# Joining 67 of 367 transfers in a four-layer FFT kernel, with a planner that knows the eight completion semaphores

## The chip, the cores and the metric

The kernel runs on one core of a Trainium2 chip. The core has a matrix engine (TensorE, called PE in the profile, with PEld for its weight loads), VectorE (DVE), ScalarE (ACT), GpSimd (POOL) and SyncE (SP), and 16 DMA engines that move data between HBM and the on-chip memories SBUF and PSUM. Each engine executes its own instructions in the order of the program and waits on semaphores for the others. The metric is the device time of one execution in microseconds (us); lower is better.

## The reference, cut to what matters

The input `x` has shape 1 x 2048 x 512 and is float32. Four layers are applied in turn, A, B, A, B, each with a layer norm ahead of it and added to its input:

```python
def A(x):                       # GFNet: a filter in the frequency domain
    return irfft2(rfft2(x, axes=(-2, -1)) * (w_r + 1j * w_i), s=(S, D))

def B(u):                       # S4: a long convolution per channel
    K = einsum("dn,dnl,dn->dl", C, exp(dt * A * arange(L)), dt * B).real
    y = irfft(rfft(pad(u.T, 2 * L)) * rfft(pad(K, 2 * L)), 2 * L)[:, :L]
    return y.T + u * Dskip

x = x + A(layernorm(x))
x = x + B(layernorm(x))
x = x + A(layernorm(x))
x = x + B(layernorm(x))
```

S = L = 2048, D = 512, and the state of B has 128 complex numbers per channel. The weights of both A layers are the same, and so are those of both B layers, so that the spectrum of K is computed once.

## The kernel before

All Fourier transforms are matmuls with small tables, done in two steps (a table of 16 or 64 points, a transposition through memory, a second table that also holds the twiddle factors). `x` (16 tiles of 128 x 512), and two large work areas `Y` and `Ya`, stay in SBUF; `wk` is an area that is cut into rings of small buffers (`RING1`, `RING2`: name, width in float32 per partition, number of buffers). PSUM is used as banks of 512 columns.

The work is cut into pieces, each a Python generator of the class `Net`. The ones that matter here:

- `first_a(r, g)` and `group_a(g)`: the column transform of A, the product with the weights and the inverse, for group g of 16. Each loads a table (`cPa`, `cGa`) and its weights (`W1`, `W`) with a transfer of its own, into one buffer `G`. `inv_a(r, s2)` is the last step of A for one of 16 tiles; in the first layer it loads `x` again (L732, 256 KB per tile), since the tile was used as workspace.
- `exp_k`, `unit_k` build the kernel K (L1127 and L1187 on PE, L1143 Exp and L1157 to L1163 Sin on ACT, L1159 to L1171 on DVE, L1174 on POOL). ACT has one function table at a time: the profile shows an `ACT_TABLE_LOAD` where Exp, Sin and the Sqrt of the layer norm (L498) follow each other. `store_k(q)` stores a quarter of K to HBM (`kd`), and `turn_k(q, i)` loads it transposed (L1235, four loads of 256 KB with 512-byte runs), does the first step of its transform (L1253 on PE), copies the result (L1268 DVE, L1270 ACT) and stores it to `yk` (L1274, issued on ACT). The last quarter is handled within layer B, with `load_t`.
- `spectra_k(q)` loads `yk` (L837, two of 256 KB), does the second step (L826 on PE, by `spectrum`), copies (L846) and stores the spectrum to `khat` (L847, on ACT, two of 256 KB).
- `forward_b(r, b, e)`: layer norm and first step of B's transform (L793 on PE, L795 on ACT) for one half e of the channels; the result goes to `Y` (e = 0) or `Ya` (e = 1) by a transfer that is issued by SP for even b and by ACT for odd b (L811). `group_b(r, q, e)`: second step (L826), product with `khat` (L921 on DVE, L927 on POOL), back (L938 on PE, L947 on ACT). In the first B layer, e = 1, it also makes the second half of the spectrum from `yk` (L898, L906, L907) with tables that `load_g` has loaded (L866, eight of 128 KB). `inv_b(r, b, e)`: the rows come back by L957 (SP for even b, ACT for odd b), then L965 on PE, L971 on DVE.

What sets the order: the class `Clock` is a list scheduler that runs while the program is built. Every `yield` of a piece names the engines and the ring buffers that its next step needs. `time` says when they will be free, `run` takes, among the steps that are ready within 0.1 us of the earliest, the one with the lowest rank, and `note` moves the planner's clocks on by a cost per instruction (`COST`), and for a transfer by its bytes at a fixed rate plus a fixed landing time. The program order that results is then fixed.

One rule is not in the planner before the change. There are eight completion semaphores for transfers (the program calls them `DMAHW0` to `DMAHW7`; below: lanes). The transfers of both issuing queues, SP's and ACT's, take them in turn, in program order. A transfer can therefore be issued only when the eighth one ahead of it, from whichever queue, has landed. An ACT issue that waits for this holds up all that follows on ACT, its computation too.

## Time and profile before

| | |
|---|---|
| time, median of 3 runs | 803.64 us (803.43 to 808.02) |
| time of the profiled execution | 801.81 us |
| its span, first to last instruction | 800.0 us |
| granted TensorE clock, mean | 0.944 |
| PE busy | 648.6 us (81%) |
| DVE busy | 510.2 us (64%) |
| ACT busy | 419.5 us (52%) |
| POOL busy | 306.5 us (38%) |
| DMA | 132.51 MB, mean 166 GB/s |
| transfers in the program | 367 |

The profile is one execution, taken by the hardware profiler. Its page gives the busy time of each engine, the span in 40 slices of 20 us, the DMA queues, the chain of work that ended last, and the costliest groups of instructions. A row of a timeline has the start, the busy time, the engine, the line of the kernel, the operation, output <- inputs, the shape and a count; the bracket at its end is the idle time of that engine just ahead, with what ended it. `ACTq` and `SPq` are the issues of transfers on these two queues. The row names an output by its area (`wk`, `Y`, `Ya`, `x`, `ps` for PSUM).

### The profile page before, as it was taken

The page shows a single profiled execution, that of the slowest core. Times are in us where ns is not written, and L with a number is a line of the kernel's source. Part 1 is how long each engine was busy: PE and PEld are TensorE (multiplying, and loading weights), DVE is VectorE, ACT ScalarE, POOL GpSimd, SP SyncE. Part 2 cuts the span into 40 slices and gives each one's busy share as a digit, 9 for nine tenths or more (in the row PEclk, how much of TensorE's full clock was granted, in tenths as well). Part 3 has the DMA queues.
Part 4 walks back from the last instruction along what each step waited for, and adds up shares of the span by engine and source line. Part 5 has one row for each costly group of instructions (what it writes and reads, how often), then busy time and mean ns, then how long its engine had stood idle before and what let it go on. Part 6 is the DMA issues. An engine that isn't in the chain of part 4 may idle for free. (4 is left out here: it accounts for less than half of the span.)

```text
span 800.0 us, 23463 instructions
## 1 busy us (share of the span) xinstructions
PE 648.6 (81%) x9892; PEld 419.3 (52%) x9892; DVE 510.2 (64%) x1022; ACT 419.5 (52%) x767; POOL 306.5 (38%) x339
## 2 busy tenths in 40 slices
PE   4389888967899799888858887889887898788796
PEld 4377555535456344346423453777665554444465
DVE  5975667747748594885525454886767588466532
ACT  5765898886886957845232324175533233433130
POOL 4290336516425340320314325264544554075420
PEclk9699999997999999999898999999997999999999
DMA  9217212630624668547986783940664524866839
GB/s 325 60 59 274 89 47 84 192 96 14 217 80 151 233 205 244 181 133 165 259 219 194 193 246 131 255 174 1 232 218 139 186 56 107 186 195 160 257 89 281
DMA packets 85960, 132.51 MB, mean 166 GB/s; under 512 B 5756, under 2 KB 57728, under 8 KB 85216
## 3 DMA queue, kind: packets, MB, share of 16 engines
q1 hardware_dynamic: 51424, 93.26, 38.3%
q10 hardware_dynamic: 34432, 37.76, 16.6%
q8 instruction: 78, 1.28, 0.7%
q14 instruction: 26, 0.21, 0.1%
HBM read 70.31 MB, written 27.13 MB: 122 GB/s over the span
## 5 line engine op out<-in xcount | busy, mean ns | idle before, releaser
L1174 POOL TENSOR_TENSOR Y<-wk,Y 128x1024 f32<-128x1024 f32 x32 | 64.8, 2027 | 120.5 <-issue 70.6
L927 POOL TENSOR_TENSOR wk<-wk 128x512 f32<-128x512 f32 x32 | 40.0, 1274 | 111.5 <-DVE wk L921 110.4
L965 PE MATMUL ps<-wk,cRbT 64*128 64x256 f32 x512 | 61.4, 384 | 5.5 <-DMA wk<-Ya 3.5
L921 DVE TENSOR_TENSOR wk<-ps,Y 128x512 f32<-128x512 f32 x64 | 39.5, 682 | 40.7 <-PE ps L826 34.8
L795 ACT COPY wk<-ps 128x512 f32<-128x512 f32 x64 | 37.1, 587 | 52.7 <-PE ps L793 45.4
L1159 DVE SCALAR_TENSOR_TENSOR wk<-wk,ps 128x1024 f32<-128x1024 f32 x32 | 38.9, 1216 | 40.5 <-ACT wk L1157 40.4
L793 PE MATMUL ps<-wk,cRb 128*32 128x256 f32 x1024 | 60.1, 380 | 4.4 <-DVE wk L515 2.8
L1127 PE MATMUL ps<-wk,Y 96*128 96x512 bf16 x128 | 44.0, 422 | 24.1 <-DVE Y L1170 13.9
L938 PE MATMUL ps<-wk,Y 32*32 32x256 f32 x1344 | 40.0, 415 | 24.7 <-ACT Y L947 9.3
L965 PEld LDWEIGHTS ps<-wk,cRbT 64*128 64x128 f32 x512 | 51.8, 187 | 15.1 <-issue 5.6
L558 PE MATMUL ps<-cRa,wk 128*128 128x256 f32 x128 | 36.6, 411 | 28.1 <-POOL wk L540 24.8
L921 DVE TENSOR_TENSOR Y<-ps,wk 128x512 f32<-128x512 f32 x64 | 39.6, 683 | 26.1 <-issue 17.5
L793 PEld LDWEIGHTS ps<-wk,cRb 128*32 128x32 f32 x1024 | 37.9, 109 | 28.2 <-DVE wk L515 3.4
L1187 PEld LDWEIGHTS ps<-Y 128*32 128x32 f32 x2048 | 36.4, 125 | 27.8 <-issue 12.8
L1143 ACT ACTIVATE Y<-ps 128x1024 f32<-128x1024 f32 x48 | 46.3, 1030 | 7.3 <-PE ps L1127 7.1
L1187 PE MATMUL ps<-Y 128*32 128x64 f32 x2048 | 42.0, 243 | 9.1 <-ACT wk L676 2.5
L947 ACT COPY Ya<-ps 128x256 f32<-128x256 f32 x64 | 19.3, 385 | 56.5 <-PE ps L938 42.9
L1170 DVE TENSOR_TENSOR Y<-ps,Y 128x1024 f32<-128x1024 f32 x32 | 39.0, 1218 | 13.0 <-ACT ps L1163 12.9
L742 PE MATMUL ps<-cDaT,apart 128*32 128x256 f32 (+1 forms) x256 | 46.3, 328 | 0.5 <-DVE x L770 0.3
L971 DVE TENSOR_TENSOR x<-x,ps 128x256 f32<-128x256 f32 x64 | 24.8, 408 | 32.9 <-PE ps L965 32.8
L540 POOL TENSOR_TENSOR wk<-wk 128x256 f32<-128x256 f32 x32 | 25.9, 808 | 49.6 <-ACT wk L513 43.9
L927 POOL TENSOR_TENSOR wk<-Y 128x512 f32<-128x512 f32 x22 | 27.5, 1276 | 45.1 <-DVE Y L921 40.1
(218 smaller groups left out, 1649.9 us busy)
## 6 DMA issues: line engine op xcount, KB each, us to landing
yk<-wk ACTq DMA_DIRECT2D x32, 256.0 KB
wk<-khat SPq DMA_DIRECT2D x16, 512.0 KB
Y<-in_W_dram SPq DMA_DIRECT2D x12, 515.0 KB
x<-in_cPa_dram SPq DMA_DIRECT2D x16, 384.0 KB
Y<-in_cGa_dram SPq DMA_DIRECT2D x12, 384.0 KB
x<-in_W_dram SPq DMA_DIRECT2D x16, 258.0 KB
x<-in_A_x_dram SPq DMA_DIRECT2D x8, 512.0 KB
kd<-wk SPq DMA_DIRECT2D x4, 1024.0 KB
```

The costliest lines, as they stand in the source:

```text
L742: nc.tensor.matmul(p[32 * i:32 * i + 32, o:o + n], self.folded(r, i)[:, b, s2].rearrange("p g m -> p (g m)"), self.DaT[:, b, first:first + ...
L793: self.nc.tensor.matmul(p[o:o + 32, 256 * h:256 * h + 256], self.Rb[:, 2 * h + j, 32 * a:32 * a + 32], xn[s], start=True, stop=True)
L921: nc.vector.tensor_tensor(t[c][:, j], x, kh[:, j, ::-1, :] if c else kh[:, j], op=OP.mult)
L927: nc.gpsimd.tensor_tensor(Z[:, :, c], t[0][:, :, c], t[1][:, :, c], op=op)
L938: nc.tensor.matmul(v[j][h][i:i + 32], gi[o:o + 32, j, 4 + 2 * s + c, :], Z[o:o + 32, j, c, :], start=c == 0, stop=c == 1)
L965: nc.tensor.matmul(q[s], self.RbT[o, i, :], y[o, i, :], start=i == 0, stop=i == 3)
L1127: self.nc.tensor.matmul(p, f[:, c:c + 128], self.oh[:k, o:o + 512], start=True, stop=True)
L1143: nc.scalar.activation(m[:, :, 1024:] if i == 2 else m[:, i, :1024], p.rearrange("p (i m) -> p i m", i=2) if i == 2 else p, AF.Exp)
L1159: nc.vector.scalar_tensor_tensor(s, c, MAGIC, p, op0=OP.subtract, op1=OP.subtract)
L1170: nc.vector.tensor_tensor(E[:, 1, :1024], p, m[:, :1024], op=OP.mult)
L1174: nc.gpsimd.tensor_tensor(E[:, 0, :1024], c, m[:, :1024], op=OP.mult)
L1187: nc.tensor.matmul(pk[32 * j:32 * j + 32, 64 * e:64 * e + 64], E1[:, r, i, :], E2[:, r, i], start=r == 0, stop=r == 1)
```

## The change

Two things are changed together.

First, 67 of the 367 transfers are joined with a neighbour. Table and weights of a group of A lie in one array on the host and come with one load (17 `PA`, 15 `GA`); `x` is loaded again two tiles at a time (8 of 512 KB for 16 of 256 KB); `turn_k` takes its input from a new piece, `load_kt`, with two loads of 512 KB (1 KB runs) for four; `spectra_k` has one load of 512 KB for two and one store of 512 KB for two; `load_g` loads its eight tables by 4, 3 and 1. The rings `KT` and `yh` have two buffers of 1024 for four of 512.

Second, the planner keeps the landing times of the last eight transfers (`self.lanes`). In `note` a transfer starts no earlier than the first of them; in `time` a step that needs SP waits for as many of them as it has transfers on SP. A transfer on ACT is moved on in `note` alone. The planner also measures a buffer's place by the size of its type.

```diff
-RING1 = {"yd": (1024, 5), "oh": (1280, 1), "KS": (2048, 1), "KT": (512, 4), "yh": (512, 4), "gb": (256, 3), "st": (256, 2), "sk": (128, 1)}
+RING1 = {"yd": (1024, 5), "oh": (1280, 1), "KS": (2048, 1), "KT": (1024, 2), "yh": (1024, 2), "gb": (256, 3), "st": (256, 2), "sk": (128, 1)}
...
+        self.lanes = last.lanes if last else [0.0] * 8
...
                 both = all(str(a.space) != str(DRAM) for a, _ in aps)
+                start = max(start, self.lanes[0])
                 self.land = max(self.land, start) + out.nbytes() / RATE[both]
                 done = self.land + LAND
+                self.lanes = self.lanes[1:] + [done]
...
-            ready = max([ready, *(self.free.get(k, 0.0) for k in words if k in COST)])
+            ready = max([ready, *(self.free.get(k, 0.0) for k in words if k in COST), *self.lanes[:words.count("SP")]])
...
-        nc.sync.dma_start(ca, self.io["cGa"][g])
+        nc.sync.dma_start(G, self.io["GA"][g])
         W = G[:, 768:1796].rearrange("p (r s f) -> p r s f", r=2, s=2)
-        nc.sync.dma_start(G[:, 768:1798], self.io["W"][g])
...
-        yield "SP" if not r else "PE", self.after(("group", r), 16)
-        if not r:
-            nc.sync.dma_start(xs, self.io["A_x"].rearrange("b (p s) d -> p (b s) d", p=128)[:, s2, :])
-            self.mark("again", s2)
+        yield "SP" if not r and s2 % 2 == 0 else "PE", self.after(("group", r), 16)
+        if not r and s2 % 2 == 0:
+            two = slice(s2, s2 + 2)
+            nc.sync.dma_start(self.x[:, two, :], self.io["A_x"].rearrange("b (p s) d -> p (b s) d", p=128)[:, two, :])
+            self.mark("again", s2 // 2)
...
-        for j in range(2):
-            nc.sync.dma_start(y[j], self.yk[0, 2 * q + j].rearrange("c a b h d -> (c a b) h d"))
+        nc.sync.dma_start(y.rearrange("p g h d -> p g (h d)"), self.yk[0, 2 * q:2 * q + 2].rearrange("g c a b h d -> (c a b) g (h d)"))
...
         for j in range(2):
-            nc.scalar.copy(kh[j].rearrange("p r d -> p (r d)"), p[j])
-            nc.scalar.dma_start(self.khat[:, 2 * q + j, :, :256], kh[j])
+            nc.scalar.copy(kh[:, j].rearrange("p r d -> p (r d)"), p[j])
+        nc.scalar.dma_start(self.khat[:, 2 * q:2 * q + 2, :, :256], kh)
...
-    def load_g(self, q):
+    def load_g(self, q, n):
...
+        nc.sync.dma_start(self.wk[:, o:o + 256 * n].rearrange("p (q m) -> p q m", q=n),
+                               self.io["cGk"][q:q + n].rearrange("q p a b m -> p q (a b m)"))
...
+    def load_kt(self, q, i):
+
+        nc = self.nc
+        yield "SP KT", self.after(("stored", q))
+        t = self.kt[q, i] = self.w("KT", [128, 4, 256])
+        self.timer.keep(t)
+        nc.sync.dma_start(t, self.kd[q].rearrange("j (a s) d -> a j (s d)", s=16)[:, :, 256 * i:256 * i + 256])
...
-            KT = self.w("KT", [128, 4, 128])
-            nc.sync.dma_start(KT, kd[:, :, 128 * i:128 * i + 128])
+        KT = self.KT3[:, :, 128 * i:128 * i + 128] if last else self.kt[q, i // 2][:, :, 128 * (i % 2):128 * (i % 2) + 128]
...
-        for q in range(8):
-            yield 0, self.load_g(q)
+        for q, n in ((0, 4), (4, 3), (7, 1)):
+            yield 0, self.load_g(q, n)
```

The order of the instructions moves where the planner decides otherwise. POOL keeps its order. DVE, ACT and PE differ in the stretches that lie, by the times of before, at about 148 to 180 us, 224 to 272 us, 290 to 366 us, 409 to 428 us and 452 to 472 us; from about 475 us on these three engines keep theirs, and only SP's list has the joined loads. The lines of after are 3 to 16 higher than those of before (L811 is L814, L947 is L955, L1270 is L1284, L1274 is L1288, L826 is L829, L938 is L946, L965 is L973).

ACT where the last quarter of K is transformed, beside the first group of `group_b` (about 404 to 428 us). `Ya<-wk` is a store of `forward_b`, `yk<-wk` one of `turn_k`, and `Y<-ps` the copy that empties the PSUM banks of L938. Before:

```order
L795 COPY wk<-ps 128x512 x4
L811 DMA Ya<-wk 16x8x1024
L947 COPY Y<-ps 128x256 x4
L795 COPY wk<-ps 128x512 x2
L1274 DMA yk<-wk 512x1x128
L811 DMA Ya<-wk 16x8x1024
L1274 DMA yk<-wk 512x1x128
L947 COPY Y<-ps 128x256 x4
L1270 COPY wk<-ps 128x4x128
L1274 DMA yk<-wk 512x1x128 x2
L947 COPY Y<-ps 128x256 x4
```

and now:

```order
L798 COPY wk<-ps 128x512 x4
L814 DMA Ya<-wk 16x8x1024
L955 COPY Y<-ps 128x256 x4
L798 COPY wk<-ps 128x512 x2
L1288 DMA yk<-wk 512x1x128 x2
L955 COPY Y<-ps 128x256 x4
L1284 COPY wk<-ps 128x4x128
L1288 DMA yk<-wk 512x1x128
L955 COPY Y<-ps 128x256 x4
L1288 DMA yk<-wk 512x1x128
L1284 COPY wk<-ps 128x4x128
L1288 DMA yk<-wk 512x1x128 x2
```

The second `Ya<-wk`, which stood between the two stores to `yk`, now comes behind all of these rows, as the next one.

ACT at the last spectra of the first half and the transform of the third quarter of K (about 279 to 310 us); `khat<-wk` is the store of `spectra_k`. Before:

```order
L1157 ACTIVATE wk<-ps,magic 128x1024
L846 COPY wk<-ps 128x512
L847 DMA khat<-wk 128x2x256
L846 COPY wk<-ps 128x512
L847 DMA khat<-wk 128x2x256
L1157 ACTIVATE wk<-ps,magic 128x1024
L746 COPY wk<-ps 128x512
L1162 ACTIVATE wk<-wk,quarter 128x1024
L1163 ACTIVATE ps<-wk 128x1024
```

and now:

```order
L1165 ACTIVATE wk<-ps,magic 128x1024
L848 COPY wk<-ps 128x512 x2
L849 DMA khat<-wk 128x4x256
L1165 ACTIVATE wk<-ps,magic 128x1024
L749 COPY wk<-ps 128x512
L1170 ACTIVATE wk<-wk,quarter 128x1024
L1171 ACTIVATE ps<-wk 128x1024
```

Two stores became one, behind both copies. Some 10 rows further on, ACT has now a pair of Sin instructions with a table load of its own (`L1170 ACT_TABLE_LOAD`) between the Sqrt of the layer norm and the Exp group; this pair stood ahead of the Sqrt before, so that ACT has one table load more in all.

PE at the rows that come back for layer B (about 450 to 472 us); L965 is the matmul of `inv_b`. Before:

```order
L826 MATMUL ps<-wk 32x256 x16
L938 MATMUL ps<-wk,Y 32x256 x32
L826 MATMUL ps<-Ya,Y 32x256 x16
L965 MATMUL ps<-wk,cRbT 128x256 x32
L938 MATMUL ps<-wk,Y 32x256 x32
L826 MATMUL ps<-wk 32x256 x16
L938 MATMUL ps<-wk,Y 32x256 x32
L826 MATMUL ps<-Ya,Y 32x256 x16
L965 MATMUL ps<-wk,cRbT 128x256 x8
L938 MATMUL ps<-wk,Y 32x256 x32
```

and now:

```order
L829 MATMUL ps<-wk 32x256 x16
L973 MATMUL ps<-wk,cRbT 128x256 x8
L829 MATMUL ps<-Ya,Y 32x256 x16
L973 MATMUL ps<-wk,cRbT 128x256 x24
L946 MATMUL ps<-wk,Y 32x256 x32
L829 MATMUL ps<-wk 32x256 x16
L946 MATMUL ps<-wk,Y 32x256 x32
L829 MATMUL ps<-Ya,Y 32x256 x16
L946 MATMUL ps<-wk,Y 32x256 x64
L973 MATMUL ps<-wk,cRbT 128x256 x8
```

The first 32 L965 are split in 8 and 24, and the first L938 moved behind them; further on 8 L965 changed places with 32 L938.

More of the change, by code (lines that the diff above doesn't have):

```diff
@@ L265, in boxes @@
         step = min([a for a, _ in rest], default=1)
+        size = mybir.dt.size(ap.dtype) / 4
         return [(p, max(1, s // width), n, low * size, step * size, (low + span) * size) for low in lows]
@@ L666, in first_a @@
         ca = G[:, :768].rearrange("p (a b) -> p a b", a=6)
-        nc.sync.dma_start(ca, self.io["cPa"][g])
+        nc.sync.dma_start(G, self.io["PA"][g])
         W = G[:, 768:1284].rearrange("p (a b) -> p a b", a=2)
-        nc.sync.dma_start(W, self.io["W1"][g])
         yield "PE p:t y", self.after(("forward", r), 16), *((self.emitted(("loaded", 0, 1), 8),) if r else ())
@@ L764, in inv_a @@
         self.drop(Y4)
-        yield "DVE" if r else ("DVE", self.after(("again", s2)))
+        yield "DVE" if r else ("DVE", self.after(("again", s2 // 2)))
         two = xs.rearrange("p (a b) -> p a b", a=2)
@@ L831, in spectra_k @@
         nc = self.nc
-        yield "SP KT KT gb", self.after(("turn", 0), 8)
+        yield "SP KT gb", self.after(("turn", 0), 8)
         gb = self.w("gb", [128, 2, 4, 32])
         nc.sync.dma_start(gb, self.io["cGk"][q])
-        y = [self.w("KT", [128, 2, 256]) for _ in range(2)]
-        for j in range(2):
-            nc.sync.dma_start(y[j], self.yk[0, 2 * q + j].rearrange("c a b h d -> (c a b) h d"))
-        yield "PE p:k yh yh"
-        kh = [self.w("yh", [128, 2, 256]) for _ in range(2)]
+        y = self.w("KT", [128, 2, 2, 256])
+        nc.sync.dma_start(y.rearrange("p g h d -> p g (h d)"), self.yk[0, 2 * q:2 * q + 2].rearrange("g c a b h d -> (c a b) g (h d)"))
+        yield "PE p:k yh"
+        kh = self.w("yh", [128, 2, 2, 256])
         p = self.psum("k")
         p = p[:, :512], p[:, 512:]
-        self.spectrum(gb, y, p)
-        self.drop(gb, *y)
+        self.spectrum(gb, [y[:, j] for j in range(2)], p)
+        self.drop(gb, y)
         yield "ACT"
         for j in range(2):
-            nc.scalar.copy(kh[j].rearrange("p r d -> p (r d)"), p[j])
-            nc.scalar.dma_start(self.khat[:, 2 * q + j, :, :256], kh[j])
+            nc.scalar.copy(kh[:, j].rearrange("p r d -> p (r d)"), p[j])
+        nc.scalar.dma_start(self.khat[:, 2 * q:2 * q + 2, :, :256], kh)
         self.mark("khat", q)
@@ L859, in tables @@
             self.mark("gi", r, q)
-    def load_g(self, q):
-        yield "SP gk", self.emitted(("rows", 0, 1), 8)
-        gk = self.gk[q] = self.w("gk", [128, 2, 4, 32])
-        self.timer.keep(gk)
-        self.nc.sync.dma_start(gk, self.io["cGk"][q])
-        self.mark("gk")
-        yield self.emitted("gk", q + 1)
+    def load_g(self, q, n):
+        yield "SP" + " gk" * n, self.emitted(("rows", 0, 1), 8)
+        t = [self.w("gk", [128, 2, 4, 32]) for _ in range(n)]
+        o = t[0].offset % WORK
+        for i in range(n):
+            self.gk[q + i] = t[i]
+            self.timer.keep(t[i])
+            assert t[i].offset % WORK == o + 256 * i
+        self.nc.sync.dma_start(self.wk[:, o:o + 256 * n].rearrange("p (q m) -> p q m", q=n),
+                               self.io["cGk"][q:q + n].rearrange("q p a b m -> p q (a b m)"))
+        for _ in range(n):
+            self.mark("gk")
+        yield self.emitted("gk", q + n)
     def early(self, q):
@@ L1222, in load_t @@
         self.mark("last")
+    def load_kt(self, q, i):
[4 more added lines that the diff above has]
+        nc.sync.dma_start(t, self.kd[q].rearrange("j (a s) d -> a j (s d)", s=16)[:, :, 256 * i:256 * i + 256])
+        if i == 0:
+            yield "+SP sk"
+            self.sk[q] = self.w("sk", [1, 128])
+            self.timer.keep(self.sk[q])
+            nc.sync.dma_start(self.sk[q], self.io["B_Dskip"].rearrange("(q a d) -> q a d", q=4, a=1)[q])
+        self.mark("kt", q, i)
     def turn_k(self, q, i):
         nc = self.nc
-        kd = self.kd[q].rearrange("j (a s) d -> a j (s d)", s=16)
         last = q == 3
-        if last:
-            yield self.emitted("last")
-            KT = self.KT3[:, :, 128 * i:128 * i + 128]
-        else:
-            yield "SP KT", self.after(("stored", q))
-            KT = self.w("KT", [128, 4, 128])
-            nc.sync.dma_start(KT, kd[:, :, 128 * i:128 * i + 128])
-        if i == 0:
-            if last:
-                sk = self.sk3
-            else:
-                yield "SP sk"
-                sk = self.w("sk", [1, 128])
-                nc.sync.dma_start(sk, self.io["B_Dskip"].rearrange("(q a d) -> q a d", q=4, a=1)[q])
-            yield ("DVE", self.after("last")) if last else "DVE"
-            o = KT[0:1, :, 0:32]
+        came = "last" if last else ("kt", q, i // 2)
+        yield self.emitted(came)
+        KT = self.KT3[:, :, 128 * i:128 * i + 128] if last else self.kt[q, i // 2][:, :, 128 * (i % 2):128 * (i % 2) + 128]
+        if i == 0:
+            yield "DVE", self.after(came)
+            o, sk = KT[0:1, :, 0:32], self.sk3 if last else self.sk[q]
             nc.vector.tensor_tensor(o, o, sk.rearrange("p (j d) -> p j d", j=4), op=OP.add)
-        yield ("PE p:x p:x", self.after("last")) if last else "PE p:k"
+            if not last:
+                self.drop(sk)
+        yield "PE p:x p:x" if last else "PE p:k", self.after(came)
         if last:
@@ L1252, in turn_k @@
         for h in range(2):
-            nc.tensor.matmul(p[h], self.Rk[:, h, :], KT if last else KT.rearrange("p j m -> p (j m)"), start=True, stop=True)
-        if not last:
-            self.drop(KT)
+            nc.tensor.matmul(p[h], self.Rk[:, h, :], KT, start=True, stop=True)
+        if not last and i % 2:
+            self.drop(self.kt[q, i // 2])
         for h in range(2):
             if not last:
-                yield "ACT yh"
-                r = self.w("yh", [128, 4, 128])
+                yield "ACT" if h else "ACT yh"
+                y = y if h else self.w("yh", [128, 2, 4, 128])
+                r = y[:, h]
             elif not h:
@@ L1275, in turn_k @@
                                 .rearrange("g c a d -> (g c) a d"), r)
-            if not last:
-                self.drop(r)
+            if not last and h:
+                self.drop(y)
             yield "+"
@@ L1287, in plan_k @@
         M, KS = {}, {}
+        self.kt, self.sk = {}, {}
         self.F, self.th = self.w("F", [128, 2, 2, 512]), self.w("th", [128, 512])
@@ L1303, in plan_k @@
                 for i in range(4 if b < 7 else 0):
+                    if i % 2 == 0:
+                        yield 4 * b + 6 + i, self.load_kt(b // 2, i // 2)
                     yield 4 * b + 6 + i, self.turn_k(b // 2, i)
@@ L1475 @@
     arrays = {"A_x": np.ascontiguousarray(A_x), "B_Dskip": np.ascontiguousarray(B_Dskip),
-              "W": host_w(A_w_r, A_w_i), "W1": host_w1(A_w_r, A_w_i),
               **host_k(B_A_re, B_A_im, B_B_re, B_B_im, B_C_re, B_C_im, B_log_dt),
               **tables_a(), **tables_b(), **table_k()}
+    for name, table, w in (("GA", "cGa", host_w(A_w_r, A_w_i)), ("PA", "cPa", host_w1(A_w_r, A_w_i))):
+        arrays[name] = np.concatenate([arrays.pop(table).reshape(16, 128, 768), w.reshape(16, 128, -1)], 2)
     nc = bacc.Bacc("TRN2", target_bir_lowering=False, num_devices=1, dynamic_dma_scratch_size=4096)
```

## The prediction

> **What bounds the kernel now.** I read the page's busy times and slices first, then the waits of PE, then the timeline at the longest wait that the change touches.

> ```profile
> span 800.0 us, 23463 instructions
> PE 648.6 (81%) x9892; PEld 419.3 (52%) x9892; DVE 510.2 (64%) x1022; ACT 419.5 (52%) x767; POOL 306.5 (38%) x339
> PEclk9699999997999999999898999999997999999999
> DMA  9217212630624668547986783940664524866839
> ```

> PE is busy for 648.6 of 800.0 us (so it waits for 151), and no other engine comes near it in most slices. The end follows PE, so time is won where PE waits or where its clock is below full, and a transfer saved elsewhere is worth nothing. The waits of PE by what ended them (sum, times, longest):

> ```profile
> PE ps L558 <- POOL wk L540: 24.8, 3, 13.1
> PE ps L1127 <- DVE Y L1170: 13.9, 7, 3.2
> PE ps L938 <- ACT Y L947: 9.7, 5, 8.3
> PE ps L826 <- DMA Y<-wk: 6.3, 2, 3.2
> PE ps L965 <- DMA wk<-Ya: 3.5, 5, 0.9
> PE ps L1127 <- DMA wk<-in_cGk_dram: 1.8, 1, 1.8
> ```

> The largest is the start, which the edit leaves as it is. Direct waits on transfers are small, and hardly any is on a transfer that gets joined (`Y<-wk` and `wk<-Ya` stay as they are). So what the joins save on SP and on the DMA engines is mostly hidden already. The one long wait in the middle is on a copy of ACT, 8.3 us. The timeline there:

> ```profile
> 405.93 5.58 SPq L895 DMA_DIRECT2D Y<-khat  x4
> 408.19 1.50 PE L938 MATMUL ps<-wk,Y 32*32 32x256 f32 x64
> 408.94 0.68 ACTq L811 DMA_DIRECT2D Ya<-wk  x1
> 409.61 1.98 PE L1253 MATMUL ps<-wk,cRk 128*128 128x512 f32 x4
> 411.56 2.83 SPq L866 DMA_DIRECT2D wk<-in_cGk_dram  x3
> 418.84 0.53 ACTq L1274 DMA_DIRECT2D yk<-wk  x1
> 419.41 1.20 ACT L947 COPY Y<-ps 128x256 f32<-128x256 f32 x4 [10.50 <-DMA Ya<-wk]
> 419.92 2.91 PE L938 MATMUL ps<-wk,Y 32*32 32x256 f32 x64 [8.33 <-ACT Y L947]
> 422.76 3.78 PE L1253 MATMUL ps<-wk,cRk 128*128 128x512 f32 x4
> ```

> The copies at 419.41 need only PE's L938 of 408.19. What held ACT is the issue ahead of them: the `yk` store at 418.84 waits for the `Ya` store of 408.94, which lies on the lane that this store gets, and which takes 9.9 us because four loads of 512 KB from `khat` went out around it. PE, whose PSUM banks wait for the copies, stands still for 8.33 us, and then runs slowly. The same stretch in windows of 4 us (PE, PEld, DVE, ACT, POOL, granted clock, DMA share, GB/s):

> ```profile
> 408.00:412.00 4.00, 3.59 (x76) 1.50 (x68) 1.29 (x3) 0.59 (x1) 2.49 (x2) 1.00 1.02 231
> 412.00:416.00 4.00, 0.00 (x0) 0.00 (x0) 0.33 (x1) 0.00 (x0) 0.00 (x0) 1.00 1.11 311
> 416.00:420.00 4.00, 0.08 (x4) 0.11 (x8) 0.00 (x0) 0.59 (x3) 0.00 (x0) 0.53 1.06 293
> 420.00:424.00 4.00, 4.00 (x66) 2.35 (x67) 0.00 (x0) 2.30 (x8) 0.00 (x0) 0.50 1.04 308
> 424.00:428.00 4.00, 4.00 (x59) 1.59 (x66) 0.93 (x2) 0.59 (x1) 0.00 (x0) 0.69 0.06 16
> 428.00:432.00 4.00, 2.64 (x56) 0.75 (x40) 4.00 (x8) 0.00 (x0) 1.58 (x2) 1.00 0.50 135
> ```

> The granted clock falls to 0.53, 0.50 and 0.69 behind the idle stretch, and the DMA engines are full until 424 us and nearly idle after.

> **Part 1, 409 to 426 us.** In the new order on ACT both `yk` stores come ahead of the copies, and the `Ya` store behind all six `yk` stores. Counting eight back in the new program, the first `yk` store behind the copies gets the lane of a `Ya` store that SP issues before its `khat` loads, the next two those of `yk` stores of the same stretch, the next that of the first `khat` load. None of these is the late `Ya` store. So the wait of 8.33 us goes, and with it the slow stretch: L938 x64 took 2.91 us where it took 1.50 before the stop (1.41), and L1253 x4 3.78 for 1.98 (1.80). Together 8.33 + 1.41 + 1.80 = 11.5 us, the upper end.

> What is late next is the `khat` data. The windows from 408 to 424 move 4 x (231 + 311 + 293 + 308) = 4.57 MB, and the next products, L921 on DVE, need the first two of the four loads. Each 512 KB takes 1.7 to 2.3 us at these rates; going by the order of issue I estimate the second at 418 us and the last at 421 (between 414 and 424). With PE 11.5 us earlier DVE wants the second at about 418.6 and the last two from about 421. That is just met; with the `yk` stores, which now share the DMA engines (256 KB each, 0.9 us at 293 GB/s), it may be missed by 0 to 5 us. I take 1.5, the nearer to "just met": **-10** (-11.5 to -6). The `Ya` store that was moved back is wanted by L826 only here:

> ```profile
> 446.33 1.36 PE L826 MATMUL ps<-Ya,Y 64*32 64x256 f32 x32
> ```

> That is 27 us behind the copies of 419.41; with the 9.9 us that it took it is still early. If its own lane, that of the second `khat` load, isn't free, ACT stops there for about a microsecond, with the 16 copies of the next group behind it; PE comes to the banks of these some 4 us later, so this is covered.

> [...]

> **Part 2, 253 to 345 us.** Here `spectra_k`, the reload of `x` and the building of K run side by side. Stretch, busy times as above:

> ```profile
> 148.00:253.00 105.00, 86.07 (x1231) 52.53 (x1230) 71.35 (x109) 81.79 (x100) 47.00 (x35) 0.92 0.35 109
> 253.00:345.00 92.00, 79.00 (x1256) 38.77 (x1248) 63.87 (x114) 68.51 (x86) 29.45 (x20) 0.96 0.66 211
> 280.00:300.00 20.00, 19.42 (x310) 9.51 (x308) 18.07 (x37) 10.14 (x14) 8.21 (x6) 0.92 0.63 205
> ```

> ```profile
> 282.75 0.37 ACTq L847 DMA_DIRECT2D khat<-wk  x1
> 283.16 0.59 ACT L846 COPY wk<-ps 128x512 f32<-128x512 f32 x1 [1.86 <-DMA x<-in_A_x_dram]
> 285.91 1.12 ACT L1157 ACTIVATE wk<-ps,magic 128x1024 f32<-128x1024 f32 x1 [2.16 <-DMA x<-in_A_x_dram]
> 299.74 1.28 ACT L498 ACT_TABLE_LOAD   x1 [0.59 <-ACT wk L1270]
> ```

> ACT loses two waits of its `khat` stores for loads of `x` (1.86 and 2.16; with eight loads for sixteen the eighth one ahead is older). Sixteen `khat` stores become eight; at 0.37 us for an issue that is 8 x 0.37 = 3.0. One table load comes in, 1.28. On ACT that is 1.86 + 2.16 + 3.0 - 1.28 = 5.7 us. But PE is busy for 19.42 of the 20 us around these waits, so there they cost nothing; PE's idle time in the whole stretch is 92 - 79 = 13 us, and ACT, with 68.5 of 92, is only sometimes what it waits for. I take a third, **-2**. Ends: if all of ACT's time is on the path and a clock dip goes with it, -7; if the table load and its pair of Sin instructions come between PE and the Exp group, +3 (1.28, and a dip of 1.5 us as at 474 us in part 4). The loads for `turn_k` are fewer and of the same bytes, behind the same loads of `x`; no PE wait on them is among the waits above.

> **Part 3, 148 to 253 us.** PE is busy for 86.07 of 105 and ACT for 81.79. Some unit steps change places; no wait of a lane is removed here and no work added but the joins. The waits for L1170 above are up to 3.2 us, and could move either way: **0** (-4 to +3), one such wait with its dip.

> **Part 4, 440 to 475 us.** L965 is split, and L938 comes later or earlier by one group.

> ```profile
> 440.00:476.00 36.00, 29.65 (x670) 17.01 (x670) 17.43 (x36) 9.87 (x26) 10.58 (x9) 0.93 0.84 237
> 454.33 1.37 PE L938 MATMUL ps<-wk,Y 32*32 32x256 f32 x50 [1.43 <-issue]
> 467.52 1.49 PE L938 MATMUL ps<-wk,Y 32*32 32x256 f32 x64
> 474.15 2.40 PE L938 MATMUL ps<-wk,Y 32*32 32x256 f32 x64 [2.19 <-POOL wk L927]
> 476.48 1.67 PE L826 MATMUL ps<-wk 64*32 64x256 f32 x32
> 477.94 1.08 PE L826 MATMUL ps<-Ya,Y 64*32 64x256 f32 x32
> ```

> At 454 PE stands before an L938 while L965 could have run, 1.43 us. In the new order it runs. The wait of 2.19 at 474 cost more than itself: 2.40 for 1.49 and 1.67 for 1.08 follow, so 2.19 + 0.91 + 0.59 = 3.7. Against a gain: DMA is at 0.84, and rows that come back later would hold the early L965. I take **-1** (-4 to +2).

> [...]

> **The rest.** The joined `GA` and `PA` loads save 32 issues on SP; no wait of PE for them is among the waits listed, and the weights, which came last, still do. The cover is the lead of several groups; without it the later landing of a 900 KB load would cost a microsecond or two per group. From 475 us on the three compute engines keep their order: **0** (-0.5 to +1).

> **Sum.** -10 - 2 + 0 - 1 + 0 = -13 on 801.81: 788.8. The median of the runs shown is 803.64, 1.8 above the profiled execution, so 790.6 for a median.

> **Rivals.**

> *The gain at 411 us is given back.* DMA is above 1.0 from 408 to 424, so what it carries ends no earlier. If the next stage waits for it, PE's hole only moves behind L826, and keeps the dip: of 11.5 us some 3 remain, the rest is -3: 803.6 - 6 = 798. For it: four loads of `khat` sit in that queue. Against: the DMA share is 0.06 right after, and only half the loads are wanted at once.

> *The other stretches gain too.* If the upper ends of parts 2 to 4 come half true (-3.5 - 2 - 2) with -11.5, it is -19: 784.6. For it: many waits of 2 to 3 us each with a slow stretch behind. Against: ACT's gain lies where PE is busy.

> *Joined transfers pay by themselves.* If fixed costs of transfers were on the path, all waits of PE for DMA in the list (6.3 + 3.5 + 1.8 = 11.6) could go: 790.6 - 11.6 = 779. Against: those transfers aren't joined. [...]

> *A new wait for a lane on ACT: slower.* The planner makes only steps on SP wait for lanes before it picks them; ACT's issues are picked as before. A joined load holds its lane longer, and where an ACT store lands eight behind one in a full stretch (440 to 475 us, share 0.84; or 345 to 404), the event of 418.84 comes back with its price of 11.5 us. One such takes the gain away (790.6 + 11.5 = 802), two make it slower: 813.6. It decides when ACT's wait outlasts PE's supply, a few us. For it: the stores of L957 and L907 on ACT stand there close behind loads. Against: ACT is busy for 9.87 of 36 us there, so it has room.

> *The change doesn't do what it says*: the late lane is met by another of the stores, and the wait stays. Then 803.6 - 3 = 800.6.

> **How the numbers follow.** Forecast (faster, 786 to 795): 0.48. More gains: 0.14. Joins pay: 0.03. Given back: 0.12, half of it above 795.6. Not done: 0.06. New wait on ACT: 0.17, of it 0.07 about level and 0.10 slower. One per cent of 803.64 is 8 us, about what a measurement of this kernel can tell from no change; so faster means under 795.6, slower over 811.7. Faster: 0.48 + 0.14 + 0.03 + 0.06 = 0.71; within: 0.06 + 0.06 + 0.07 = 0.19; slower: 0.10. The range takes in the forecast with the ends of its parts and both milder rivals: 778 to 804.

> **What would show it.** Right: no `yk` store on ACT with a wait of several us near 410, L938 behind it at 1.5 us for 64, granted clock 1.0 in that stretch, L1253 of the last quarter ending 10 us earlier relative to the stretch before; the waits of `khat` stores for `x` gone; ACT's busy time about 1 us more by the table load. Wrong: a wait of L921 on `Y<-khat` of over 3 us, a new wait of ACT on a DMA of over 3 us, or PE waits for L1143 behind the moved Sin pair. The prediction falls if the stretches before 400 us, whose order moved most, differ by more than 5 us.

## The result, and the profile after

The changed kernel takes 794.6 us in the median of 20 runs, the one before 803.3 us. The ratio is 0.988, with a 95% interval of 0.986 to 0.991 (all ratios leave out runs over 1.5% above the fastest of their kernel: 4 of these 20, 2 of 6 on the second occasion, 5 of the 10 of `joins_only` below). On the second occasion, on one chip with the kernel before, it was 0.982 (0.978 to 0.986). The profiled execution has a span of 788.8 us, 11.2 less than before; a single execution of this kernel may lie 10 us off another. The forecast was 790.6 in a range of 778 to 804.

The page after: busy times, and waits of PE by what ended them (sum, times, longest). L829 is L826 of before, L946 is L938, L955 is L947, L1135 and L1178 are L1127 and L1170.

```profile
span 788.8 us, 23367 instructions
PE 651.1 (83%) x9892; PEld 420.5 (53%) x9892; DVE 508.4 (64%) x1022; ACT 419.9 (53%) x768; POOL 304.1 (39%) x339
```

```profile
PE ps L829 <- issue: 14.8, 7, 4.6
PE ps L1135 <- DVE Y L1178: 10.3, 5, 2.5
PE ps L946 <- ACT Y L955: 1.5, 4, 0.4
PE ps L946 <- issue: 1.0, 2, 0.9
```

The same kind of rows before:

```profile
PE ps L938 <- issue: 9.5, 6, 2.5
PE ps L826 <- issue: 2.2, 2, 1.3
```

The 8.3 us behind ACT's copy are gone (9.7 in all before, 1.5 now). L826 on "issue", 2.2 us before, is now the second largest, 14.8 us; but L938 on "issue" went from 9.5 to 1.0, and one of the seven waits in the 14.8 (4.07 us at 687.05) is of another kind, as shown below. Without that one and those under 0.7 us, the waits on issue make 11.2 us before and 11.4 after: there are not more of them in all, they stand elsewhere. The timeline at the place of part 1:

```profile
402.18 1.50 PE L946 MATMUL ps<-wk,Y 32*32 32x256 f32 x64
402.33 1.96 ACTq L1288 DMA_DIRECT2D yk<-wk  x2
404.32 1.20 ACT L955 COPY Y<-ps 128x256 f32<-128x256 f32 x4 [1.42 <-PE ps L946]
405.52 1.49 PE L946 MATMUL ps<-wk,Y 32*32 32x256 f32 x64
406.95 1.98 PE L1266 MATMUL ps<-wk,cRk 128*128 128x512 f32 x4
408.86 2.15 PE L829 MATMUL ps<-Y 64*32 64x256 f32 x64
```

From the first L946 to the L829 are 6.7 us, where it was 18.3. And the stretch that part 4 speaks of, where the gain was partly lost again:

```profile
447.26 0.66 PE L829 MATMUL ps<-Ya,Y 64*32 64x256 f32 x14
452.49 1.86 PE L829 MATMUL ps<-Ya,Y 64*32 64x256 f32 x18 [4.57 <-issue]
454.27 2.37 PE L946 MATMUL ps<-wk,Y 32*32 32x256 f32 x64
457.71 2.40 PE L946 MATMUL ps<-wk,Y 32*32 32x256 f32 x64 [1.06 <-ACT Ya L955]
460.51 4.05 PE L973 MATMUL ps<-wk,cRbT 64*128 64x256 f32 x16 [0.40 <-ACT Ya L955]
464.49 1.79 PE L829 MATMUL ps<-wk 64*32 64x256 f32 x32
```

```profile
444.00:448.00 4.00, 3.92 (x148) 1.75 (x118) 0.00 (x0) 2.81 (x9) 0.00 (x0) 1.00 1.02 261
448.00:452.00 4.00, 0.00 (x0) 0.00 (x0) 0.00 (x0) 0.66 (x3) 0.00 (x0) 1.00 1.02 250
452.00:456.00 4.00, 3.51 (x80) 1.59 (x81) 2.26 (x4) 0.00 (x0) 0.00 (x0) 0.54 0.93 328
456.00:460.00 4.00, 2.88 (x94) 0.58 (x64) 0.22 (x1) 1.20 (x4) 2.49 (x2) 0.50 0.13 44
460.00:464.00 4.00, 3.60 (x31) 3.33 (x16) 0.00 (x0) 1.20 (x4) 0.00 (x0) 0.50 0.00 0
```

In the middle of a row of equal matmuls PE stops for 4.57 us, with DMA full (1.02), and the granted clock is 0.54 to 0.50 for the next 12 us.

To see where time goes in many kernels, I counted matmuls by line in each trace and noted when the same one begins. M1 is the 1024th L1187, M2 the 257th L826, M3 the 400th, M4 the 513th (the first L826 on `wk`), M5 the 769th. Each column is the time between two of them, in us, for one profiled execution; "issue" is the sum of waits of over 0.7 us that the profile gives to issue between M4 and M5. Kernels below the line are the experiments.

```
                  M1-M2   M2-M3   M3-M4   M4-M5   issue M4-M5
before            187.6    40.4    17.9    31.9       1.4
changed           181.5    29.7    15.3    40.0       7.0
changed_again     182.9    28.8    14.9    40.5       6.5
------------------------------------------------------------
late_store        186.8    28.8    15.0    36.7       5.7
joins_only        182.2    33.0    16.7    34.7       1.3
lanes_only        197.0    32.2    18.0    34.3       1.0
order_450_again   182.1    29.4    15.4    40.5       8.0
shift_128         183.1    28.1    14.9    41.3       6.8
shift_128_again   185.6    29.1    15.2    42.4       8.1
shift_64          185.4    30.3    19.4    37.5       4.9
small_store       184.8    27.9    14.9    39.5       5.4
few_rows          185.9    28.3    15.8    42.0       8.3
split_spectra     185.3    29.0    15.4    42.5       7.8
```

Up to M1 the changed kernel is 0.8 us ahead, and behind M5 it neither wins nor loses. The kernel before has one profile; `late_store` has its order up to M2, so that 187.6 and 186.8 are two executions of the old order there.

### The profile page after: what moved, and what is told of

It is laid out like the page before. It is cut to its first block, busy times and chain, and to the rows that moved or that the text cites. A ratio compares the mean times of both kernels' runs of the same rounds, so it can differ in the third digit from the quotient of the medians.

```text
span 788.8 us, 23367 instructions
## 1 busy us (share of the span) xinstructions
PE 651.1 (83%) x9892; PEld 420.5 (53%) x9892; DVE 508.4 (64%) x1022; ACT 419.9 (53%) x768; POOL 304.1 (39%) x339
## 3 DMA queue, kind: packets, MB, share of 16 engines
q8 instruction: 78, 1.28, 0.7%
## 5 line engine op out<-in xcount | busy, mean ns | idle before, releaser
L973 PE MATMUL ps<-wk,cRbT 64*128 64x256 f32 x512 | 64.5, 397 | 6.1 <-DMA wk<-Ya 3.7
L929 DVE TENSOR_TENSOR wk<-ps,Y 128x512 f32<-128x512 f32 x64 | 39.5, 684 | 37.3 <-PE ps L829 29.0
L1135 PE MATMUL ps<-wk,Y 96*128 96x512 bf16 x128 | 44.7, 431 | 22.7 <-DVE Y L1178 10.3
L973 PEld LDWEIGHTS ps<-wk,cRbT 64*128 64x128 f32 x512 | 54.3, 195 | 16.7 <-issue 7.3
L929 DVE TENSOR_TENSOR Y<-ps,wk 128x512 f32<-128x512 f32 x64 | 39.5, 684 | 24.7 <-issue 14.0
L979 DVE TENSOR_TENSOR x<-x,ps 128x256 f32<-128x256 f32 x64 | 24.8, 408 | 42.7 <-PE ps L973 42.5
L955 ACT COPY Ya<-ps 128x256 f32<-128x256 f32 x64 | 19.3, 386 | 60.0 <-PE ps L946 43.8
L1178 DVE TENSOR_TENSOR Y<-ps,Y 128x1024 f32<-128x1024 f32 x32 | 39.0, 1219 | 17.4 <-ACT ps L1171 17.4
L946 PE MATMUL ps<-wk,Y 32*32 32x256 f32 x1344 | 38.4, 411 | 7.3 <-POOL wk L935 3.6
```

The source lines that it names most:

```text
L929: nc.vector.tensor_tensor(t[c][:, j], x, kh[:, j, ::-1, :] if c else kh[:, j], op=OP.mult)
L946: nc.tensor.matmul(v[j][h][i:i + 32], gi[o:o + 32, j, 4 + 2 * s + c, :], Z[o:o + 32, j, c, :], start=c == 0, stop=c == 1)
L973: nc.tensor.matmul(q[s], self.RbT[o, i, :], y[o, i, :], start=i == 0, stop=i == 3)
L1135: self.nc.tensor.matmul(p, f[:, c:c + 128], self.oh[:k, o:o + 512], start=True, stop=True)
L1178: nc.vector.tensor_tensor(E[:, 1, :1024], p, m[:, :1024], op=OP.mult)
```

## Experiments

**The place of one store.** `late_store` is the kernel before with one edit:

```diff
-        yield "SP"
+        yield ("SP", self.emitted(("turn", 1), 8)) if (r, b, e) == (0, 7, 1) else "SP"
```

> The kernel before with one edit: the last odd store of forward_b (b = 7, e = 1) waits in the planner until all stores of turn_k are placed, so that it stands on ACT behind the six yk stores, as in the changed kernel. PE's order is that of before. If the place of this one store made the wait of 8.33 us, the wait goes and the stretch from the first L938 there to the next L826 takes 6.7 us as in the changed kernel (18.3 before), 11.6 us less; if the joined gk load or the lighter queue did it, a wait of over 3 us stays. Behind it (445 to 475 us of before) the order is that of before: if the 8 us that the changed kernel lost there come from its new order, this kernel keeps its gain and ends 11 to 13 us under before (a profile of about 789); if they come from reaching that stretch earlier, it loses 5 to 8 us there and ends 4 to 7 us under before.

Measured: 0.994 of before (0.989 to 0.998); span 789.8 us. The place in its timeline:

```profile
407.75 1.49 PE L938 MATMUL ps<-wk,Y 32*32 32x256 f32 x64
407.89 1.30 ACTq L1274 DMA_DIRECT2D yk<-wk  x2
409.23 1.20 ACT L947 COPY Y<-ps 128x256 f32<-128x256 f32 x4 [0.76 <-PE ps L938]
411.09 1.49 PE L938 MATMUL ps<-wk,Y 32*32 32x256 f32 x64
412.51 1.98 PE L1253 MATMUL ps<-wk,cRk 128*128 128x512 f32 x4
414.43 2.38 PE L826 MATMUL ps<-Y 64*32 64x256 f32 x64
```

From 407.75 to 414.43 are 6.7 us, as in the changed kernel, with the three single loads of `gk` and PE's order of before. M2 to M3 takes 11.6 us less. So the place of this one store is enough, and all of the slow stretch goes with the wait. Behind it this kernel loses 4.8 us between M4 and M5 though its order there is that of before. That much of the loss in that stretch therefore does not need the new order; it came with reaching the stretch earlier.

**Joins and planner apart.** `joins_only` is the changed kernel without the planner's two conditions:

```diff
-                start = max(start, self.lanes[0])
...
-            ready = max([ready, *(self.free.get(k, 0.0) for k in words if k in COST), *self.lanes[:words.count("SP")]])
+            ready = max([ready, *(self.free.get(k, 0.0) for k in words if k in COST)])
```

> The changed kernel with the planner's two lines on lanes taken out: the transfers are joined, the planner doesn't know of lanes. On ACT the late Ya store stands between the yk stores again, as before. If the place of the store matters and not the transfers themselves, a wait of 6 to 9 us with its slow stretch is back at about 405 us. The gain of 5.5 us that the changed kernel has between 253 and 408 us stays if it comes from the fewer khat stores and x loads, and goes to within 2 us of nothing if it comes from the order. In all 0 to 6 us under before.

`lanes_only` is the kernel before with the planner's lines put in, and no transfer joined:

```diff
+        self.lanes = last.lanes if last else [0.0] * 8
...
+                start = max(start, self.lanes[0])
...
+                self.lanes = self.lanes[1:] + [done]
...
-            ready = max([ready, *(self.free.get(k, 0.0) for k in words if k in COST)])
+            ready = max([ready, *(self.free.get(k, 0.0) for k in words if k in COST), *self.lanes[:words.count("SP")]])
```

> The kernel before, all 367 transfers single, with the planner's lines on lanes put in. On ACT the late Ya store stands ahead of the yk stores, so the wait at about 410 us should stay (6 to 9 us and the slow stretch). If the order is what won 5.5 us between 253 and 408 us, this kernel has most of that; if the joins did it, it has none. In all 0 to 6 us under before, and over the changed kernel in any case.

Measured: `joins_only` 0.987 (0.983 to 0.991), but that is half of its runs; the median of all ten, 796.9, is 0.994 of the 801.4 of before. So it is faster than before, and whether it is as fast as the changed kernel is not shown. `lanes_only` 1.010 (1.003 to 1.017, four runs), slower than before, where I had expected 0 to 6 us less. The place in `joins_only`, with the `Ya` store between the `yk` stores as before:

```profile
403.06 0.75 ACTq L813 DMA_DIRECT2D Ya<-wk  x1
404.27 2.32 SPq L871 DMA_DIRECT2D wk<-in_cGk_dram  x1
406.74 0.53 ACTq L1287 DMA_DIRECT2D yk<-wk  x1
407.32 1.20 ACT L954 COPY Y<-ps 128x256 f32<-128x256 f32 x4 [4.28 <-DMA Ya<-wk]
407.83 2.91 PE L945 MATMUL ps<-wk,Y 32*32 32x256 f32 x64 [2.12 <-ACT Y L954]
```

I had expected 6 to 9 us here; PE waits 2.12. One load of `gk` instead of three moves the count of eight back by two: the second `yk` store now gets the lane of the `Ya` store that SP issued at 399.07, and not of the one at 403.06. So there were two ways to the same gain: the moved store takes all of the 11.6 us without any join, and the joins take 7.4 of it between M2 and M3 without the moved store. That it is the `gk` join among them follows from the count; it wasn't run alone.

`lanes_only` lost 9.4 us between M1 and M2. At M2 the profile gives a wait to a load from `khat`:

```profile
394.89 1.54 PE L829 MATMUL ps<-Y 64*32 64x256 f32 x24 [8.22 <-DMA Y<-khat]
```

The name misleads. The two `khat` loads of that moment land at 399.2 and 402.0 us, when these matmuls are under way. What lands just ahead of them, at 394.65, is the last store to `Y`, which ACT issued at 380.44. The kernel before waits at the same matmul for the same store, issued at 374.17 and landed at 386.23:

```profile
386.36 3.67 PE L826 MATMUL ps<-Y 64*32 64x256 f32 x64 [3.16 <-DMA Y<-wk]
```

So this wait grew by 5.1 us; the other waits of the stretch are together 0.6 shorter, and PE's busy time grew by 5.1 us, at a granted clock of 0.948 for 0.970. The wait of part 1 shrank to 3.76 us there; PE came to the place 9 us later. The planner's new knowledge alone made the order worse. The gain of some 6 us between M1 and M2 that the changed kernel's own profile shows is in `joins_only` too (5.4).

**The transfers of the spectra.** `split_spectra` has `spectra_k`'s loads and stores single again, in joined buffers:

```diff
-        nc.scalar.dma_start(self.khat[:, 2 * q:2 * q + 2, :, :256], kh)
+            nc.scalar.dma_start(self.khat[:, 2 * q + j, :, :256], kh[:, j])
```

(and the same for `yk`). In the order that follows, one buffer of `KT` is handed on before `turn_k(2, 0)` has read it, so that this one step of K's transform works on other data; instructions and shapes are the same.

> The changed kernel, with the transfers of spectra_k single again (two loads of yk, two stores of khat; the buffers stay joined). If the fewer khat stores on ACT won the 6 us that the changed kernel gained between 200 and 386 us of before, most of that goes: the point at 386 us of before comes 0 to 3 us early instead of 6.9. If the other joins (x, the loads of turn_k) won it, 5 to 7 us stay.

Measured: 0.991 (0.988 to 0.994). At M2 it is 3.05 us ahead of before, as expected if the spectra's joins had won most. But M1 to M2 takes 181.5 to 185.9 us in the seven executions whose order there is the changed one's (`changed`, `changed_again`, both `shift_128`, `shift_64`, `small_store`, `few_rows`), and 185.3 lies among them, with a wait of 1.86 us that the handed-on buffer itself made:

```profile
292.68 1.96 PE L1267 MATMUL ps<-wk,cRk 128*128 128x512 f32 x4 [1.86 <-DMA wk<-yk]
```

Against the two executions of the old order (187.6 and 186.8) the joins as a whole won 1 to 6 us there (5.4 in `joins_only`), 3 in the mean; which of them did it stays open.

**The stretch M4 to M5: the order.** In `order_450` the first L973 wait for the third group, so that the 32 stand together again:

```diff
+        self.mark("X", r, e, q)
...
+            *((self.emitted(("X", 0, 1, 2)),) if (r, b, e) == (0, 0, 0) else ())
```

> The changed kernel with one more condition for the planner: the first L973 of inv_b (b = 0, first B layer) comes only behind the third group's L829 on Ya, so that its 32 matmuls stand together again, as before the change. If the earlier 8 of them (which free a buffer and so let ACT issue a 512 KB load 4.6 us sooner, ahead of the block of instructions that PE then lacks) made the stop of 4.57 us and the slow stretch behind it, then the stretch from the first L829 on wk to the same point behind it takes 32 to 34 us instead of 40.0, and the kernel ends 6 to 8 us under the changed one (about 787 in a median). If the stretch is simply full of transfers, whatever the order, it stays at 38 to 41 us and the time stays within 2 us of the changed one's.

Measured: 0.983 (0.976 to 0.991). The profiled execution was the longest of the four, 801.2 us for 783.6 to 791.3, so that its trace does not count in what follows (M4 to M5 takes 41.9 us in it). I ran the kernel again:

> The kernel of order_450, once more. By the blocks of the program, the order of L973 matters little by itself: the time is within 3 us of the changed kernel's, and the stretch from the first L829 on wk to the matmuls after it takes 35 to 41 us, with waits put down to issue of 3 to 9 us. If the early L973 made it, 32 to 34 us and 6 to 8 us under the changed kernel.

Measured: 0.987 (0.981 to 0.992), M4 to M5 in 40.5 us, with this in the middle:

```profile
450.85 0.66 PE L829 MATMUL ps<-Ya,Y 64*32 64x256 f32 x14
457.73 1.86 PE L829 MATMUL ps<-Ya,Y 64*32 64x256 f32 x18 [6.22 <-issue]
```

The stop is at the same matmul and longer. My theory of the early L973 falls. The order at large is not cleared by this: in `order_450` as in the changed kernel the first L946 stands behind the L973, and not ahead of them as before.

**The stretch M4 to M5: what "issue" is.** Waits of PE on issue in the changed kernel come after PE has begun 10434, 10690, 11201, 17602, 17858 or 18369 instructions (matmuls, weight loads and PE's own instructions that wait for semaphores, 20002 in the trace): always 193 or 194 over a multiple of 256. In the kernel before they are at 10178, 10689, 17089, 17857, 18370, 18626 and 18881, with the same remainder. The page has a queue for instructions,

```profile
q8 instruction: 78, 1.28, 0.7%
```

78 transfers, in the trace of 16384 bytes each. One for every 256 instructions would be 64 bytes for each, and 78 x 256 = 19968 is nearly PE's 20002. Each wait ends 1.2 to 1.7 us behind the end of such a transfer. Over the 13 profiles of the table there are 74 waits of this kind of over 0.7 us, and all 74 stand at 193 or 194. The profile puts 17 more waits on issue, which are not of this kind: all stand at the first L826 of a B layer (the 4.07 us at 687.05 is one), where PE's own instructions, just ahead, wait for the stores to `Y`. They are left out here and below. If PE lacks its own program, the waits must move when the program is shifted. `shift_128` puts 64 matmuls on zeros ahead of it, `shift_64` 32:

```diff
+        t = self.const.tile([128, 64], F32, name="shift")
+        self.nc.vector.memset(t, 0.0)
+        for _ in range(64):
+            self.nc.tensor.matmul(self.ps[:64, 3584:3648], t, t, start=True, stop=True)
```

> The changed kernel with 64 small matmuls on a tile of zeros ahead of everything on PE (their result is overwritten and used by nobody; with their weight loads 128 instructions), in PE's idle time at the start. In the changed kernel each wait of PE that the profile puts down to issue comes when PE has begun 193 or 194 instructions more than a multiple of 256 (10434, 10690, 11201, 17602, 17858, 18369), and ends 1.3 to 1.6 us after a transfer of 16384 bytes on the instruction queue, which is 256 instructions of 64 bytes. If these waits are for blocks of the program, they come again at 193 or 194 over a multiple of 256 with the 128 counted in, so at other matmuls of the program: the stop of 4.57 us before the 11201st goes to about the 11073rd or 11329th of the old count, and changes its length. If they belong to the place in the program, they stay before the same matmul. Time within 6 us of the changed kernel's either way.

> As shift_128 with 32 matmuls (64 instructions). By the blocks: the waits come at 129 or 130 over a multiple of 256 in the old count; by the place: no change. Time within 6 us of the changed kernel's either way.

Measured: 0.984 (0.978 to 0.989) and 0.990 (0.983 to 0.997). All other waits on issue over 0.7 us of both, in the new count:

```
shift_128   10689 11458 18113 18626 18882 19137          over 256: 193 194 193 194 194 193
shift_64     9153 10433 11202 11457 17858 18114 19138    over 256: 193 193 194 193 194 194 194
```

In the old count 11458 is 11330, one of the two places foretold, and no wait is left at 11201. In the trace of `shift_128`:

```profile
444.02 0.66 PE L829 MATMUL ps<-Ya,Y 64*32 64x256 f32 x15
448.69 1.49 PE L829 MATMUL ps<-Ya,Y 64*32 64x256 f32 x17 [4.02 <-issue]
```

So these waits go with the count of PE's instructions and not with the place in the program, and each ends 1.2 to 1.7 us behind one of the 78 transfers. This settles what they are in this kernel: PE has run out of instructions, because a block of its program, one of these transfers, is late. `shift_128` looked faster than the changed kernel, so both ran on one chip:

> shift_128 once more, beside the changed kernel on the same chip. If it is truly faster than the changed kernel, by waits that fall elsewhere, its median is 4 to 8 us lower again; if that was a matter of single executions, within 3 us.

> The changed kernel, for comparison on the same chip: a ratio to before of 0.986 to 0.991. In its profile the stretch behind the first L829 on wk should again take 36 to 42 us with waits put down to issue at 193 or 194 over a multiple of 256; the length of each may differ, if it depends on what the transfer engines hold when a block is due.

Measured: 0.986 (0.982 to 0.990) and 0.982 (0.978 to 0.986). It is not faster. The changed kernel's second profile has its stops at 10434 and 11201 again, 2.18 and 4.31 us long.

**The stretch M4 to M5: why a block is late.** Between M4 and M5 DMA is full up to 456 us (a share of 0.97 at 424 to 444 us and 0.98 at 448 to 456 in the changed kernel), and a 512 KB transfer takes 12.7 to 12.9 us from issue to landing (the changed kernel, 425 to 470 us, last column the median in us):

```profile
khat<-Y ACTq DMA_DIRECT2D x6, 512.0 KB, 12.9
wk<-yk SPq DMA_DIRECT2D x5, 512.0 KB, 12.7
```

So I cut the eight stores of the stretch, first by columns, then by rows. The planner still counts them whole, so that the order stays, and the last layer loads what is stored and computes without the rest:

```diff
-            nc.scalar.dma_start(self.khat[:, two, :, d], kh)
+            nc.scalar.dma_start(self.khat[:, two, :, 256:320], kh[:, :, :, :64])
...
+            nc.scalar.dma_start(self.khat[:32, two, :, d], kh[:32])
```

> The changed kernel, of whose eight stores of the second half of the spectrum in the first B layer only 64 of 256 columns are stored (and loaded again in the last layer), so that the computation of the last layer misses the rest; the order of the instructions is that of the changed kernel. 3 MB of the 9.4 MB that move in the stretch from the first L829 on wk to 475 us fall away, about 10 us of full DMA. If the stretch is long because the blocks of the program and the loads wait behind full transfers, the waits put down to issue there shrink to under 1.5 us in all (7.0 in the changed kernel) and the stretch takes 31 to 34 us for 40.0. If the order on PE makes it long, it takes 38 to 40 us.

> As small_store, but cut by rows: only 32 of the 128 partitions of each of the eight stores are stored (and loaded again in the last layer, whose computation misses the rest), in the same runs of 1 KB; small_store cut the columns, and its short runs kept the transfer engines full (share 0.94 to 1.03 at 250 to 266 GB/s). If the blocks of instructions are late because the transfer engines are full, the share falls to 0.6 to 0.8 in the stretch behind the first L829 on wk, the waits put down to issue there shrink to under 1.5 us in all, and the stretch takes 31 to 35 us (40.0 in the changed kernel). If the blocks are late for another reason, waits of 3 us and more stay and the stretch takes 38 to 41 us.

Measured: M4 to M5 39.5 and 42.0 us, stops of 3.76 and 6.52 us. Windows of `few_rows`:

```profile
440.00:448.00 8.00, 7.85 (x136) 5.31 (x132) 5.98 (x15) 1.20 (x4) 2.50 (x2) 1.00 1.00 231
448.00:456.00 8.00, 2.12 (x86) 0.99 (x79) 0.00 (x0) 2.27 (x6) 0.00 (x0) 0.91 1.01 273
```

DMA stays full, at fewer bytes per us (231 and 273 GB/s here; the changed kernel has 300 and 289 in the same two windows), against what I expected of either cut. In `few_rows` the runs are 1 KB long as in the changed kernel, so that short runs are not what keeps it full. Neither run shows a stretch with free transfer engines, and that the fullness makes the block late is not shown. For it speaks that blocks come later where the transfer engines are full, over all 13 profiles (figures in the last section).

The traces also tell what is special about the block behind 11201. From its 10930th to its 11201st instruction PE takes 3.9 us in `changed`, `changed_again`, `order_450_again`, `split_spectra`, `small_store` and `few_rows`, which stop there for 3.8 to 6.5 us. In the new order only short matmuls (L829, L946) stand in that piece. It takes 6.7 or 6.8 us in `before`, `late_store` and `lanes_only`, where L965 stand in it, and 4.4 in `joins_only`, where the L945 ran slower. The transfer of the block starts 5.4 to 8.4 us behind the 10930th instruction in the first six, 2.4 to 4.1 in the other four. So in the new order PE uses up its supply sooner, and the block comes later as well. Why it comes later is not shown.

## Why the prediction was right, and where not

The direction, the size (13 us forecast, 11.2 in the profile and 9.3 by the ratio) and the main cause were right; one term was wrong by 9 us, and others made up for 8 of it: 4 in part 2, 2.6 in a stretch that had no term, 1.5 in parts 1 and 3. That the total came out so near is luck.

- *Part 1, -10 (-11.5 to -6).* Measured -10.7 by M2 to M3, and -11.6 from the first L938 to the L826. The upper end held, and the mechanism is the one foretold: each `yk` store behind the copies got the lane that the prediction counted out for it, by the semaphores that the issues carry in the trace, and `late_store` shows that the place of the `Ya` store alone does it. The matmuls behind the place ran at 1.49 and 1.98 us, at a granted clock of 1.00 from 402 to 409 us, so the full 3.2 us of slow stretch came back. One thing named as a sign of being wrong was there, a wait of L921 (now L929) for `khat` of 3.34 us, at 389.89, one group ahead of the place; PE waited 1.29 us behind it. The rival that gives the gain back at the next stage is out (M3 to M4 got shorter), but in `late_store`, where nothing else is new, 4.8 of the 11.6 us went again between M4 and M5. What I overlooked is that the joined `gk` load alone moves the lane count.
- *Part 2, -2 (-7 to +3).* M1 to M2 gave -6.1 in the first profile, -4.7 in the second, and -1.7 to -6.1 over executions of this order. The sign was right, and with this spread the size can't be judged closely. But the prediction said that it falls if the stretches before 400 us differ by more than 5 us. At M2 they differ by 6.9 us in the first profile and 7.8 in the second: by that sign it falls, although the range of this part took the gain in. The `khat` stores' waits for `x` are gone from ACT's list.
- *Part 3, 0.* -0.8 at M1, within its range.
- *M3 to M4*, for which I had no term, gave -2.6: the wait of 2.48 us at 441.57 in the timeline of before, one on issue, is not there.
- *Part 4, -1 (-4 to +2).* Measured +8.1. This is the step that failed. I read the wait of 1.43 us "on issue" before an L938 as an order that could be improved. It was a block of instructions that came late. In the changed kernel three blocks are late by 7.0 us together in this stretch, 5.6 more than before, and a granted clock of 0.5 follows for 12 us: PE's busy time in the stretch grew from 27.4 to 31.4 us, and its other waits shrank by 1.3. The split of L973 that I blamed at first isn't the cause (`order_450_again`); that the new order leaves less time for the block is seen, and why the block starts late stays open.
- *The rest, 0.* Right to 0.1 us from M5 to the last L965 (-12.0 at both), by luck: `changed_again` takes 1.3 us longer for the same piece.
- *The rival of a new lane wait on ACT* did not come true where I put it; `lanes_only` shows that the planner's knowledge can make the kernel slower, by a later store to `Y` on which PE waits.
- Slow matmuls came behind gaps of about 2 us too: the 2.12 us in `joins_only` are followed by L945 x64 in 2.91 us instead of 1.49, and the 2.19 us at 474 us in the profile of before by a granted clock of 0.56 and 0.58 in the two windows of 2 us from 474 us on. Part 4's reading of that wait holds.

## What to carry to other kernels

Before a wait on an engine's issue queue is blamed on bandwidth, count back to the transfer that owns the completion semaphore it gets: moving one store changed which transfer was waited for and was worth 11.6 us at the place, and joins with the store unmoved 7.4 there, while the joins as a whole won 1 to 6 us between M1 and M2. Some of what is won at one place can go again further on (4.8 of 11.6 us in `late_store`): compare the traces with and without the change to their ends. A planner that knows one more rule need not give a better order: with the transfers single it gave a worse one (1.010 of before). Where the profile says that TensorE waited on nothing, look at the count of its instructions and at the instruction queue: 74 of the 91 such waits of over 0.7 us here stand at 193 or 194 over a multiple of 256. And where it names a transfer, look whether that transfer had landed: the two `khat` loads named at 394.89 us in `lanes_only` landed 4.3 and 7.1 us later.

## What the runs showed of the hardware

Each issue of a transfer carries the number of its semaphore in the trace. The 367 issues of the kernel before use eight numbers, 45 or 46 times each, the 300 of the changed one the same eight, 37 or 38 times each, and the issues of SP and ACT together fit one round of the eight in turn. For one number, with 37 issues, the profile of the changed kernel has every landing: none of the 36 later issues begins before the one ahead of it on that number has landed, and the closest begins 0.02 us behind. In the kernel before, the `yk` store at 418.84 us has the number of the `Ya` store of 408.94, whose last event on it ahead of that is at 418.76.

Executions of one kernel differ by some 10 us, and these stops are little of it: `shift_128` and its repeat have spans of 783.3 and 791.4 us, with 13.5 and 14.3 us of such stops in all and a granted clock of 0.947 and 0.934.

None of the 367 issues in the trace of before and of the 300 in that of the changed kernel reads or writes PSUM (`ps`). Of the two on-chip memories that the first section names for the DMA engines, they serve SBUF alone here; results leave PSUM by instructions of ACT and DVE, as in the rows `Y<-ps` and `wk<-ps` (in each of the two traces 583 of ACT and 638 of DVE read `ps`).
